# One piece of w_in, not four, multiplied in plain float32, and another table of moved works

## The chip, the cores and the metric

The kernel runs on one core of one Trainium2 chip. The metric is the device time of one execution in microseconds (us). A core has engines that work side by side and wait for each other by semaphores: TensorE (PE in the profile, with its weight loads as PEld), VectorE (DVE), ScalarE (ACT), GpSimd (POOL) and SyncE (SP), whose queue issues every load and store of this kernel.

## The reference

Attention over 4 batches and 12 heads of 448 positions and width 64, causal, and then two dense layers on its output, with an ELU between them:

```python
scores = scale * np.matmul(q, k.transpose(0, 1, 3, 2))
scores = np.where(mask, -1000000000.0, scores)
attn = softmax(scores)                      # rows, with 1e-9 in the sum
attn_out = np.matmul(attn, v)
x = attn_out.transpose(0, 2, 1, 3).reshape(B * S, H * D)   # 1792 x 768
h = x @ w_in                                # 768 x 2048
g = np.where(h > 0.0, h, np.exp(np.minimum(h, 0.0)) - 1.0)
out = g @ w_out                             # 2048 x 768
```

The weights come as float64 and are turned into float32 on the core.

## The kernel before

**Tiling.** The 448 positions of a batch are cut into four chunks of 112. A token tile is one chunk index of all four batches, 448 columns; the first tile (g = 0) needs only the first chunk of queries and keys, the second one two chunks, the last two tiles ("joint") three or four. Heads are taken in six pairs p, since two heads fill 128 partitions. w_in is cut into 16 pieces f of 128 output columns, each with six blocks k of 128 rows, and block k of the first layer meets the output of head pair k.

**Stages.** `first_pair` does the attention of the first tile for one pair: loads (q0, k0, and v0 in two halves), scores `sc` (L515), softmax on VectorE (L419) and ScalarE (L423), transposes `tr` (L440), products with v `av` (L453), the spread of the reciprocal sums `rb` (L535), and `xf`, the normalised float32 result (L539). `attention(0)` and `attention(1)` do the same for the second tile and for the last two (L614, L679, L647). `layers(g)` is the first dense layer of tile g, `mixed_h` that of the last two tiles and `mixed_o` the second layer of two tiles each.

**A piece of w_in.** `load64` brings its float64 words (768 KB); `convert` makes float32 of them in five steps on VectorE and ScalarE (L736, L740, L741, L744, L747) and stores them to `kin` (L758). `in_two` then splits the piece into a high and a low part `whl`: a copy in the rounded type (L775 on ScalarE, or L776 on VectorE) and a subtraction (L778, VectorE). x is split likewise into `xh` and `xl`. A block product is then three matmuls of 448 columns in the rounded type (`three`, L817 to L819).

**PLAIN.** For tile 0 the first PLAIN pieces are not split: a block product is one float32 matmul of `xf` with the piece (L840; the trace shows two records for each). With PLAIN = 4 these are pieces 0 to 3, 24 matmuls. Pieces 0 to 2 run abreast (k outside, f inside), the others one after the other. `xf[k]` is given back after the last plain piece has met it.

**What sets the order.** Nothing is written out by hand. Every step is a "work" of a `Plan`, with an engine (or a choice of ScalarE and VectorE), an estimated cost, what it reads and writes, and a due time. `draft` places the works one after the other: of those that can start at about the same time on an engine the one wanted first is taken, and `want = due - SOONER[n]` for work number n. SOONER is the table of moved works. The order that results is fixed when the program is built; at run time each engine does its own list in that order and waits where an input is late. The same holds for the loads: SyncE issues them in the listed order, and each waits until the eighth before it has landed.

Of the kernel before, what the change touches and what calls it, by code (L numbers as in the profile page):

```python
# [108 lines left out]
class Plan:  # L109
# [21 lines left out]
    def add(self, ways, reads=(), writes=(), due=None, size=0.0, hold=(), after=None):  # L131
# [24 lines left out]
        return w  # L156

    SOONER = {
# [30 lines left out]
    }  # L189

    def rank(self):
# [124 lines left out]
def attention_moe_kernel(ctx, tc, qk, v, w_in, w_out, out):  # L316
# [42 lines left out]
    BANKS = ("hp", "p", "av", "bank")  # L359
    SHARED = {"row": sum(PLACES[x] for x in ROWS), "bank": sum(PLACES[x] for x in BANKS)}  # L360

    PLAIN = 4

    def ring(tag):
        if tag not in rings:
# [4 lines left out]
    def new(tag, shape, dtype=F32, name=None):  # L370
        pool = ps if tag in BANKS else sb
        slot = "row" if tag in ROWS else "bank" if tag in BANKS else tag
        bufs = SHARED.get(slot) or PLACES[slot]
        return ring(tag).new(lambda: pool.tile(shape, dtype, tag=slot, name=name or tag, bufs=bufs))

    def pe(cost, fn, reads, writes, due, hold=(), after=None):
        return plan.add(("PE", cost, fn, False), reads, writes, due, hold=hold, after=after)
# [29 lines left out]
    def done(*bufs):  # L407
        for b in bufs:
            b.ring.done(b)
# [356 lines left out]
    def in_two(w, n):  # L766
        t = new("w6", [P, 2, KT, P], F32R, "whl")
        hi_lo(lambda: t()[:, 0, :n], lambda: t()[:, 1, :n], lambda: w()[:, :n], n * P, (t, 0), (t, 1), w)
        done(w)
        return t, (lambda k: t()[:, 0, k]), (lambda k: t()[:, 1, k])  # L770
# [55 lines left out]
    def emit_h(g, f, k, due):  # L826
        if k == 0:
            if g == 0:
                for n in range(0 if f == 0 else f + EARLY, min(f + EARLY + 1, FT)):
                    load64(("i", n))  # L830
                w = convert(("i", f))
            elif f < FT - BOTH:
                w = fetch(f)
            if g == 0 or f < FT - BOTH:
                st["w", f] = (w,) if g == 0 and f < PLAIN else in_two(w, KT)
            st["h", f] = new("hp", [P, S], name="hp")
        hp, w = st["h", f], st["w", f]
        if len(w) == 1:
            x = xf[k]
            pe(ONE, lambda: nc.tensor.matmul(hp(), w[0]()[:, k], x(), start=k == 0, stop=k == KT - 1), [*w, x], [hp], due)  # L840
            if f == PLAIN - 1:
                done(x)
        else:
            x = xt[g, k]
            pe(THREE, lambda: three(hp, w, k, x, k == 0, k == KT - 1), [w[0], *x], [hp], due)
            if f == (FT - 1 if g == 0 else FT - 1 - BOTH):
                done(*x)
        if k < KT - 1:
            return
        if g or f < FT - BOTH:  # L850
            done(w[0])
        o = G[0, f // HALF_F, g, f % HALF_F] = row("G")
        elu(o, hp)

    def layers(g):
# [4 lines left out]
        for f, k in order:  # L860
            yield ONE if g == 0 and f < PLAIN else THREE, lambda due, f=f, k=k: emit_h(g, f, k, due)

# [367 lines left out]
```

## Time and profile before

| what | us |
|---|---|
| median of three runs | 604.09 |
| lowest and highest run | 602.19, 604.17 |
| the profiled execution | 602.11 |
| its span, from the first instruction to the last | 600.3 |
| TensorE busy in it | 588.2 |
| VectorE busy | 517.3 |
| ScalarE busy | 440.6 |

The profile is of one execution. Its span leaves out some 1.8 us of the execution's own time. A view by stage shows where an engine idles; the chain of waits runs back from the last instruction to what released each step; the timeline lists instructions by start. TensorE's matmuls overlap their neighbours, so that the durations of single rows add up to more than the time; the chain and the distances between starts do not have that fault. The clock that TensorE was granted was 0.999 of full speed over the span.

### The profile page before, as it was taken

How to read it: one execution, taken by the hardware profiler on the slowest of the kernel's cores; microseconds unless marked ns; L12 is line 12 of the kernel's file. 1: busy time of each engine (PE TensorE's matmuls, PEld its weight loads, DVE VectorE, ACT ScalarE, POOL GpSimd, SP SyncE). 2: the span in 40 equal slices, each digit the busy share in tenths (PEclk: the TensorE clock that was granted, in tenths of full speed). 3: DMA queues.
4: the chain of work that ended last, by engine and by line, in shares of the span. 5: the costliest groups of instructions: out<-in, count | busy, mean ns of one | idle time of the engine just before them, and what ended most of it. 6: DMA issues, size and time to landing. Idle time of an engine off the chain costs nothing.

```text
span 600.3 us, 11631 instructions
## 1 busy us (share of the span) xinstructions
PE 588.2 (98%) x4086; PEld 518.2 (86%) x4086; DVE 517.3 (86%) x1212; ACT 440.6 (73%) x980; POOL 1.5 (0%) x12
## 2 busy tenths in 40 slices
PE   6999999999999999999999999999999999999997
PEld 5766888888788888888888889999999999999996
DVE  4889999999999999998999897699878999998511
ACT  6999989899899989887779766258747886574300
POOL 0000000000000000000000000000000000000000
PEclk9999999999999999999999999999999999999999
DMA  9999999988999999875456588996953334451111
GB/s 228 250 346 342 374 287 316 279 240 252 327 325 298 348 318 280 278 214 169 139 166 199 156 288 256 334 329 238 319 159 106 106 105 132 117 141 53 46 48 46
DMA packets 113610, 134.36 MB, mean 224 GB/s; under 512 B 42512, under 2 KB 86800, under 8 KB 113552
## 3 DMA queue, kind: packets, MB, share of 16 engines
q1 hardware_dynamic: 113552, 133.62, 72.2%
q8 instruction: 32, 0.52, 0.4%
q14 instruction: 26, 0.21, 0.1%
HBM read 101.45 MB, written 32.15 MB: 223 GB/s over the span
## 4 chain that ended last, share of the span: by engine, by line
PE 91%; DMA 2%; ACT 2%; SPq 2%; DVE 2%; issue 0%; ACTq 0%
PE op L817 12%; PE op L819 11%; PE op L818 11%; PE hp L817 11%; PE hp L819 10%; PE hp L818 10%; PE av L647 6%; PE tr L679 6%; PE sc L614 6%; PE hp L840 3%; DMA v<-in_v 1%; DMA w<-kin 1%; SPq L500 1%; PE av L453 1%; SPq L505 1%; ACT a L423 1%
## 5 line engine op out<-in xcount | busy, mean ns | idle before, releaser
L775 ACT ACTIVATE whl<-w 128x768 fp32r<-128x768 f32 x102 | 85.4, 842 | 75.5 <-PE op L819 41.2
L817 PE MATMUL op<-ph,whl 128*128 128x448 f32 (+1 forms) x338 | 126.4, 374 | 0.0
L819 PE MATMUL op<-ph,whl 128*128 128x448 f32 (+1 forms) x338 | 123.1, 364 | 0.0
L818 PE MATMUL op<-pl,whl 128*128 128x448 f32 (+1 forms) x338 | 123.1, 364 | 0.0
L778 DVE TENSOR_TENSOR whl<-w,whl 128x768 fp32r<-128x768 f32 x108 | 102.4, 953 | 14.4 <-ACT whl L775 14.0
L423 ACT ACTIVATE a<-a,nm 112x336 f32<-112x336 f32 (+3 forms) x192 | 98.0, 522 | 11.9 <-DVE nm L419 11.7
L419 DVE CUSTOM_DVE_ANT_0 a<-sc,mask 112x336 f32<-112x336 f32 (+3 forms) x192 | 74.7, 443 | 9.3 <-PE sc L515 7.4
L817 PEld LDWEIGHTS op<-ph,whl 128*128 128x128 f32 x338 | 63.5, 188 | 8.8 <-issue 3.8
L819 PEld LDWEIGHTS op<-ph,whl 128*128 128x128 f32 x338 | 63.5, 188 | 5.2
L818 PEld LDWEIGHTS op<-pl,whl 128*128 128x128 f32 x338 | 63.6, 188 | 4.5
L817 PE MATMUL hp<-xh,whl 128*128 128x448 f32 x168 | 65.6, 390 | 0.0
L819 PE MATMUL hp<-xh,whl 128*128 128x448 f32 x168 | 61.4, 366 | 0.0
L818 PE MATMUL hp<-xl,whl 128*128 128x448 f32 x168 | 61.4, 366 | 0.0
L818 PE MATMUL hp<-pl,whl 128*128 128x448 f32 x168 | 61.4, 365 | 0.0
L817 PE MATMUL hp<-ph,whl 128*128 128x448 f32 x168 | 61.4, 365 | 0.0
L819 PE MATMUL hp<-ph,whl 128*128 128x448 f32 x168 | 61.3, 365 | 0.0
L679 PE MATMUL tr<-ident,a 112*112 112x112 f32 x432 | 50.2, 259 | 0.5 <-DVE nm L419 0.4
L679 PEld LDWEIGHTS tr<-ident,a 112*112 112x112 f32 x432 | 45.1, 133 | 5.8 <-DVE nm L419 1.1
L683 ACT ACTIVATE at<-tr 112x448 f32<-112x448 f32 (+1 forms) x109 | 47.5, 497 | 1.5 <-PE tr L679 1.5
L647 PEld LDWEIGHTS av<-at,v 112*64 112x64 f32 x864 | 41.5, 137 | 5.5 <-issue 3.1
L647 PE MATMUL av<-at,v 112*64 112x112 f32 x864 | 45.4, 261 | 0.0
L913 ACT ACTIVATE m<-hp 128x448 f32<-128x448 f32 x56 | 30.2, 538 | 13.9 <-DVE hp L908 7.0
(96 smaller groups left out, 990.4 us busy)
## 6 DMA issues: line engine op xcount, KB each, us to landing
w<-kin SPq DMA_DIRECT2D x40, 384.0 KB, 5.4
w<-in_w_in SPq DMA_DIRECT2D x16, 768.0 KB, 9.1
w<-in_w_out SPq DMA_DIRECT2D x24, 512.0 KB, 6.3
w<-sout SPq DMA_DIRECT2D x32, 384.0 KB, 3.4
w<-kout SPq DMA_DIRECT2D x24, 384.0 KB, 3.2
qk<-in_qk SPq DMA_DIRECT2D x24, 336.0 KB, 5.3
kin<-w SPq DMA_DIRECT2D x16, 384.0 KB, 7.1
sout<-w SPq DMA_DIRECT2D x12, 512.0 KB, 5.6
```

The source lines that it names most:

```text
L419: plan.add(dve(n, lambda: nc.vector.tensor_tensor_reduce(out=a()[:, c], in0=sc()[:, c], in1=mask[:, S - n:], op0=ALU.add, op1=ALU.min, sca ...
L423: plan.add(act(n, lambda: nc.scalar.activation(a()[:, c], a()[:, c], AF.Exp, bias=nm()[:, x:x + 1], scale=-1.0, accum_out=su()[:, x:x + 1] ...
L614: nc.tensor.matmul(sc[half]()[:, lo:lo + n], s["q"](d, x), s["k"](d, y, n), start=i == 0, stop=i == len(s["split"]) - 1,)
L647: nc.tensor.matmul(av()[half_of(half), chunk(u % 4)], o["v"][1](half, i), at()[:, chunk(x)], start=i == 0, stop=i == chunks(u) - 1,)
L679: nc.tensor.transpose(tr()[:, chunk(x)], a[:, chunk(i)], ident)
L683: act(w, lambda: nc.scalar.activation(at()[:, :w], tr()[:, :w], AF.Copy)),
L775: act(n, lambda: nc.scalar.activation(h(), x(), AF.Copy), 0.09),
L778: sub = lambda eng: lambda: eng.tensor_tensor(out=l(), in0=x(), in1=f32(h()), op=ALU.subtract)
L817: nc.tensor.matmul(acc(), wh(k), xh(), start=first, stop=False, skip_group_check=more)
L818: nc.tensor.matmul(acc(), wh(k), xl(), start=False, stop=False, skip_group_check=more)
L819: nc.tensor.matmul(acc(), wl(k), xh(), start=False, stop=last, skip_group_check=more)
L913: plan.add(act(S, lambda: nc.scalar.activation(m(), h(), AF.Relu, scale=-1.0)), [h], [m])
```

## The change

PLAIN goes from 4 to 1, so that pieces 1, 2 and 3 are split for tile 0 like the others: 18 float32 matmuls go (24 to 6), 54 matmuls in the rounded type come, and three splits. `xf[k]` is given back after piece 0. Since the works are numbered in order of their making, and three splits are two works each, the numbers behind them shift; the table SOONER is another one, of 240 entries, and moves works all over the program.

```diff
     SOONER = {
-        0: 284.3, 1: 284.4, 7: -8.8, 12: 1.9, 14: -2.2, 15: -3.8, 17: 0.4, 21: -14.5, 23: -45.2, 31: 0.6,
...
+        0: 160.1, 1: 164.8, 2: 11.8, 3: 8.8, 5: -12, 6: 1.7, 10: 0.6, 15: -43, 16: -1.2, 21: -2.8, 29: 3.3, 32: 2,
...
     }
...
-    PLAIN = 4
+    PLAIN = 1
```

Lines behind the table stand four lines higher in the changed kernel (L840 is L836 there). Three places show what the table does.

**The loads at the start**, SyncE's queue. In the kernel before, from the sixth load on (q and k are the first tile's queries and keys of a pair, v a half of its values, w a piece of w_in):

```order
L500 DMA k_104<-in_qk 128x4x112
L505 DMA v_106<-in_v 112x4x64 x2
L500 DMA q_109<-in_qk 128x4x112
L500 DMA k_111<-in_qk 128x4x112
L505 DMA v_127<-in_v 112x4x64
L500 DMA q_129<-in_qk 128x4x112
L500 DMA k_131<-in_qk 128x4x112
L728 DMA w_133<-in_w_in 128x1536
L505 DMA v_151<-in_v 112x4x64 x2
L505 DMA v_127<-in_v 112x4x64
L500 DMA q_182<-in_qk 128x4x112
L500 DMA k_189<-in_qk 128x4x112
```

The same stretch of the changed kernel, down to the last of the first tile's queries:

```order
L724 DMA w_106<-in_w_in 128x1536
L496 DMA q_108<-in_qk 128x4x112
L496 DMA k_110<-in_qk 128x4x112
L501 DMA v_112<-in_v 112x4x64 x2
L496 DMA q_115<-in_qk 128x4x112
L501 DMA v_131<-in_v 112x4x64 x2
L724 DMA w_134<-in_w_in 128x1536
L496 DMA k_150<-in_qk 128x4x112
L724 DMA w_155<-in_w_in 128x1536
L501 DMA v_161<-in_v 112x4x64 x2
L496 DMA k_187<-in_qk 128x4x112
L496 DMA q_193<-in_qk 128x4x112
```

The first piece of w_in moved up from behind the fifth pair's q and k to the seventh place, and two more pieces now stand ahead of the last pair's q and k; before, one piece stood there.

**TensorE at the start**. In the kernel before, from the first product with v of a pair (`v_106`) to the first plain product `hp`:

```order
L453 MATMUL av<-at,v_106 64x112 x6
L535 MATMUL rb<-ident,rr_80 64x112 x8
L440 MATMUL tr<-ident,a 112x112 x8
L453 MATMUL av<-at,v_127 64x112 x8
L515 MATMUL sc<-k_131,q_129 112x112 x8
L440 MATMUL tr<-ident,a 112x112 x4
L535 MATMUL rb<-ident,rr_82 64x112 x8
L453 MATMUL av<-at,v_151 64x112 x8
L535 MATMUL rb<-ident,rr_83 64x112 x8
L440 MATMUL tr<-ident,a 112x112 x4
L515 MATMUL sc<-k_189,q_182 112x112 x8
L840 MATMUL hp<-xf,w 128x448 x2
```

In the changed kernel, from the fifth pair's scores on:

```order
L511 MATMUL sc<-k_150,q_115 112x112 x8
L436 MATMUL tr<-ident,a 112x112 x4
L531 MATMUL rb<-ident,rr_81 64x112 x8
L449 MATMUL av<-at,v_131 64x112 x8
L449 MATMUL av<-at,v_161 64x112 x4
L511 MATMUL sc<-k_187,q_193 112x112 x8
L531 MATMUL rb<-ident,rr_82 64x112 x8
L449 MATMUL av<-at,v_161 64x112 x2
L531 MATMUL rb<-ident,rr_83 64x112 x8
L449 MATMUL av<-at,v_161 64x112 x2
L531 MATMUL rb<-ident,rr_80 64x112 x8
L436 MATMUL tr<-ident,a 112x112 x16
```

The last pair's scores moved ahead of the products and spreads of the pairs before it, and no plain product stands near them any more: the first one comes two products with v and one group of second-tile scores after this stretch.

**TensorE around the plain products**, `hp` of the first pieces in the changed kernel:

```order
L449 MATMUL av<-at,v_229 64x112 x8
L836 MATMUL hp<-xf,w 128x448 x5
L813 MATMUL hp<-xh,whl 128x448
L814 MATMUL hp<-xl,whl 128x448
L815 MATMUL hp<-xh,whl 128x448
```

Where before the plain products of four pieces stood between the groups of the attention, five plain products of piece 0 now stand in a row, and split products of pieces 1 and 2 follow them at once.

## Rows read from the trace of the kernel before

**Rows 1.** The page: span; busy us, share of the span and instructions by engine.

```profile
span 600.3 us, 11631 instructions
PE 588.2 (98%) x4086; PEld 518.2 (86%) x4086; DVE 517.3 (86%) x1212; ACT 440.6 (73%) x980; POOL 1.5 (0%) x12
```

**Rows 2.** Busy by stage: window, length, each engine's busy us, clock, DMA share, GB/s.

```profile
20.00:40.00 20.00, 20.00 (x202) 13.80 (x198) 17.82 (x75) 19.36 (x54) 0.00 (x0) 1.00 1.04 323
40.00:60.00 20.00, 20.00 (x110) 12.63 (x105) 18.14 (x46) 18.73 (x46) 0.00 (x0) 1.00 1.05 335
...
80.00:100.00 20.00, 20.00 (x139) 17.98 (x137) 19.31 (x47) 18.38 (x42) 0.00 (x0) 1.00 0.99 258
100.00:120.00 20.00, 20.00 (x171) 17.51 (x170) 18.95 (x63) 16.37 (x45) 0.00 (x0) 1.00 0.96 301
...
140.00:160.00 20.00, 18.74 (x158) 15.90 (x156) 19.50 (x54) 17.44 (x41) 0.00 (x0) 1.00 0.89 278
```

**Rows 3.** The chain of waits, 11 to 57 us: start, length, what.

```profile
11.83 7.63 DMA v<-in_v
...
20.49 0.97 PE sc L515 x16
...
22.91 0.77 PE av L453 x16
...
25.94 1.70 PE hp L840 x4
...
29.62 0.95 PE hp L840 x2
...
35.05 3.96 PE hp L840 x10
...
43.31 8.46 PE hp L840 x22
...
56.42 0.21 PE hp L817
56.62 0.20 PE hp L818
56.83 0.20 PE hp L819
```

**Rows 4.** Timeline of SyncE's queue: start and length of an issue, in and out.

```profile
9.66 1.12 SPq L728 DMA_DIRECT2D w<-in_w_in  x1
...
23.93 1.78 SPq L728 DMA_DIRECT2D w<-in_w_in  x1
```

**Rows 5.** DMA issues of 23.9 to 24.0 us: count, KB each, us to landing.

```profile
w<-in_w_in SPq DMA_DIRECT2D x1, 768.0 KB, 8.1
```

**Rows 6.** DMA of the first 32 us: packets, volume, mean rate, packet sizes.

```profile
DMA packets 13370, 8.00 MB, mean 250 GB/s; under 512 B 12127, under 2 KB 12893, under 8 KB 13366
```

**Rows 7.** Timeline of TensorE, 157 to 161 us, with idle time and its releaser.

```profile
157.54 0.36 PE L819 MATMUL hp<-xh,whl 128*128 128x448 f32 x1
158.22 0.41 PE L614 MATMUL sc<-qkhl 64*112 64x336 f32 x2 [0.32 <-ACT qkhl L775]
159.44 1.18 PE L614 MATMUL sc<-qkhl 64*112 64x336 f32 x10 [0.82 <-DVE qkhl L778]
160.55 0.47 PE L817 MATMUL hp<-xh,whl 128*128 128x448 f32 x1
```

**Rows 8.** The same view, 173 to 176 us.

```profile
173.70 0.55 PE L679 MATMUL tr<-ident,a 112*112 112x112 f32 x4
174.65 0.59 PE L679 MATMUL tr<-ident,a 112*112 112x112 f32 x4 [0.41 <-DVE nm L419]
175.02 0.45 PE L817 MATMUL hp<-xh,whl 128*128 128x448 f32 x1
```

**Rows 9.** Groups by line: out<-in, count, busy us, mean ns, idle before.

```profile
L778 DVE TENSOR_TENSOR whl<-w,whl 128x768 fp32r<-128x768 f32 x108 | 102.4, 953 | 14.4 <-ACT whl L775 14.0
...
L776 DVE CAST whl<-w 128x768 fp32r<-128x768 f32 x6 | 3.3, 550 | 0.0
```

54 rows, old and new, of the table SOONER are left out of this document.

## The prediction

> **What bounds the kernel now.** I read the page first: TensorE is busy for 588.2 of 600.3 us, VectorE for 517.3, ScalarE for 440.6 [rows 1]. A matmul's row overlaps its neighbours, so this alone doesn't make TensorE the bound. The view by stage says more: from 20 to 140 us TensorE has no idle time, while ScalarE and VectorE have little (19.36 and 17.82 of 20 us in the second stage); the first gap of TensorE is 1.26 us at 140 to 160 [rows 2]. The chain of waits then gives what a matmul really takes, since its steps don't overlap. It runs through a load up to 19.46 us (11.83 + 7.63) and from there on TensorE alone to beyond 57 us, with no gap between its steps [rows 3]. So from 20 us on every us of TensorE's work counts in full, and so does every us by which it starts late. Two things hold it elsewhere: the loads of the first 20 us, and short waits for VectorE and ScalarE between 157 and 175 us.
>
> The loads are the second thing to read. The third piece of w_in is issued at 23.93 us and lands 8.1 us later, at 32.0 [rows 4, 5]: the queue is that far behind its issues, and the first 32 us bring 8.00 MB at 250 GB/s [rows 6]. What is put ahead in this queue delays what comes behind it.
>
> **The change, part by part.**
>
> *Matmuls.* In the chain the 24 plain products take 3 x 1.70 + 2 x 0.95 + 3.96 + 8.46 = 19.42 us (of the steps of two and four records one each stands in [rows 3]). Six stay: the changed order has five in a row and one alone, like the steps of 3.96 and 0.95, 4.91 us. So 14.51 us go. The 54 new matmuls are 18 groups of 0.21 + 0.20 + 0.20 = 0.61 us [rows 3], 10.98 us. A first matmul behind another kind of work takes some 0.1 us more (160.55 to 160.86 where 0.20 is usual, by the next start in that view), and the order has a few more such places. I take 3.4 us saved (3.2 to 3.5). It is all TensorE's own time, thus on the path.
>
> Beside it stands a rule that speaks against this. TensorE's weight loads are busy for 12.63 of 20 us at 40 to 60 us, where the plain products are, and 86% over the span [rows 1, 2]. The Trainium skill, "Perfetto Trace Analysis", section "Identifying the Most-Contended Engine", takes the busy share of weight loads and not that of matmuls as the measure of how full TensorE is. By it TensorE would have room in that stage, and the 3.4 us would be worth nothing. The chain, in which one matmul starts when the one before it is through, disagrees; I go by the chain.
>
> *Loads at the start.* Here the table costs something. The last pair's scores need q_193, and ahead of it the changed queue has, with itself, 12 q and k of 224 KB, 6 halves of v of 112 KB and 3 pieces of 768 KB: 5664 KB. Before, 3680 KB had landed by 19.46 us (10 q and k, 6 halves, 1 piece), and 7008 KB by 32.0 us (16, 10, 3) [rows 3, 4, 5]: 265 KB per us between them. The missing 1984 KB take 7.5 us, so q_193 lands at about 26.9 us. Bounds: at the mean of [rows 6], 244 KB per us, it is 27.6; if the small loads that are no longer ahead of it cost as much per KB as those of the first 19.46 us (189 KB per us, 7.1 us for 1344 KB off 32.0), it is 24.9. I keep 26.9, which rests on the same mixture.
>
> TensorE stands behind that load, because the scores are ahead of the spreads and products that could fill the time. By the two orders, before the last pair's scores it has done 5 groups of scores, 24 transposes, 20 products with v and 16 spreads. Before the change it had done 4, 24, 16 and 16 when it began the fifth pair's scores, at 20.49 us [rows 3]. The difference is one group of scores, 0.97, and four products, half of 0.77 [rows 3]: 1.36 us. So at the same point of its work TensorE is 26.9 - 20.49 - 1.36 = 5.1 us later (3.0 to 5.8), and since it has no gaps in the kernel before from there to 140 us, nothing gives this back in that stretch.
>
> *Splits and copies.* Three subtractions of 0.953 us and, as the counts by line have it, three rounded copies of 0.550 us more on VectorE [rows 9], 4.5 us; other copies change engine the other way, and by the counts of all forms VectorE gets 2.5 us more in all and ScalarE nearly nothing. It costs nothing where TensorE is held by loads; where VectorE holds TensorE it counts.
>
> *The waits at 157 to 175 us.* From the last matmul at 157.54 to the one at 160.55 lie 3.01 us; one matmul and a dozen scores are 0.20 + 1.27 of it (a dozen without a wait, by the starts of the same view), so 1.54 is lost. From 173.70 to 175.02 eight transposes take 1.32 where 0.70 is usual: 0.6 more [rows 7, 8]. With a like place of 0.3 at 153.6 us it makes 2.4 us. TensorE now comes there with 5.1 us more of idle time behind it, which the feeding engines have too. Against it stand VectorE's additions and the moved works: I added up, with mean durations by form, VectorE's work ahead of each of TensorE's waits and TensorE's own ahead of it. Between 150 and 180 us of TensorE's work the tightest place needs 2.8 us more of VectorE, relative to TensorE, than before. With VectorE's idle time unchanged 2.4 + 2.8 - 5.1 = 0.1 us of waiting is left. So 2.3 us of the waits go. The two ends: nothing goes (0), all goes (2.4).
>
> *The rest.* The order at the end (last products, stores) is the same in kind; I take nothing for it. Earlier return of `xf` frees places in the pool of rows; no wait of TensorE in the trace points there, so nothing.
>
> *Sum.* 600.3 - 3.4 + 5.1 - 2.3 = 599.7 us span; with the 1.8 us around it 601.5. The profiled execution, 602.11, is at the low end of the runs (602.19 to 604.17, median 604.09). Taken from the median the same -0.6 us gives 603.5. Neither level is better founded, so the number is the middle, 602.5.
>
> **The rivals.**
>
> *Faster: the late load is covered.* If q_193 lands at the early bound and the moved works also feed the middle, the head costs 3.0 and all 2.4 us of waits go: -2.8 us. With a little less of either, as when TensorE's other works at the start fill more of the time than I count, it is -3.4 us and more, the whole of the matmuls' saving: 598.7 from the profiled execution. For it: the table is a whole other arrangement, and 7.5 us of load time rest on a mean rate. Against: the scores block TensorE's list until the load is there, and head and middle trade against each other, since a TensorE that comes earlier to 157 us waits there for VectorE.
>
> *Slower: ScalarE holds TensorE from 35 to 120 us.* The splits of pieces 1 and 2 and of x stand some 20 us sooner than before. Adding up as above, ScalarE's work ahead of TensorE's waits exceeds TensorE's own by at most 0.9 us before, in the first 60 us of work, and by up to 2.6 after. With ScalarE's later start (its first softmax waits for a third load instead of a second) that is just covered by the 5.1 us: the margin is about half a us. It decides from the point where ScalarE idles longer than that; before, it idled 0.6 + 1.3 us at 20 to 60 and 1.6 + 3.6 at 80 to 120 us [rows 2]. If it idles as much, 7.1 us, what is left by 110 us is some 3.8 us of waiting: 601.5 + 3.8 = 605.3.
>
> *No gain from the matmuls*, by the rule on weight loads: 601.5 + 3.4 = 604.9, less than half a per cent above 602.11.
>
> That the change doesn't do what it says is excluded by the order: 6 plain products, 18 more groups of three.
>
> **How the numbers follow.** What a measurement of this kernel can tell from no change is about 0.5%, 3 us. The forecast (-0.6; with its bounds from -2.8 to +2.6) gets 0.57, the late load covered 0.17, ScalarE 0.16, no gain from the matmuls 0.05, and 0.05 is left for what I don't see, 0.02 of it faster and 0.03 slower. Faster by over 0.5%: 0.17 + 0.02 = 0.19. Slower: 0.16 + 0.03 = 0.19. Within: 0.62. The range goes from the forecast's low bound at the profiled execution, 602.1 - 2.8 = 599.3, to its high bound near the median's level, 606.0 (604.09 + 2.6 is 606.7, but that end needs all bounds at once); it takes in the ScalarE case at the profiled level and, of the faster one, the part down to -2.8.
>
> **What would show it.** Right: the chain of the changed kernel has 6 plain products at 4.9 us; its TensorE begins the last pair's scores at 26 to 28 us behind a wait for `q`, and the first plain product at 35 to 36 us instead of 25.9; idle time of TensorE in the first 30 us is 4 to 5 us more; at 150 to 180 us there is less than 1 us. Wrong in the head: those scores before 25.5 us. Wrong in the middle: TensorE idle for over 2 us anywhere between 35 and 200 us, with ScalarE or VectorE as releaser, which would make it slower. Wrong in the matmuls: groups of three at more than 0.65 us in the first 60 us.

## The result: slower by 0.8 to 1.0%

The changed kernel took 607.33 us (median of four runs, 607.22 to 609.25) against 604.13 us before; the ratio of the fast runs is 1.0082, 95% interval [1.0062, 1.0103] (the two medians alone give 1.0053). Measured once more, later, it was 608.48 against 602.3 us, 1.0105 [1.0081, 1.0128]. Predicted were 602.5 us, from 599.3 to 606.0: the time lies outside the range and on the slower side. The profiled execution took 607.24 us, 605.5 of it span, 5.2 more than before.

The page of the changed kernel, first its line of busy times (busy us, share of the span, instructions), which answers to [rows 1]:

```profile
span 605.5 us, 11711 instructions
PE 587.2 (97%) x4104; PEld 520.5 (86%) x4104; DVE 520.9 (86%) x1217; ACT 439.5 (73%) x981; POOL 1.5 (0%) x12
```

TensorE is busy for 1.0 us less, and the span is 5.2 us longer. VectorE got 3.6 us more work (2.5 were counted). The view by stage (window, length, busy us of PE, PEld, DVE, ACT, POOL, clock, DMA share, GB/s) says where TensorE idles; it answers to [rows 2]:

```profile
0.00:20.00 20.00, 11.77 (x134) 9.44 (x135) 10.29 (x76) 12.58 (x48) 1.47 (x12) 1.00 0.98 266
20.00:40.00 20.00, 17.77 (x198) 13.88 (x198) 17.59 (x65) 20.00 (x56) 0.00 (x0) 1.00 1.01 295
40.00:60.00 20.00, 20.00 (x170) 16.76 (x168) 18.71 (x57) 19.97 (x55) 0.00 (x0) 1.00 0.96 298
...
120.00:140.00 20.00, 20.00 (x146) 17.37 (x145) 16.03 (x42) 14.14 (x31) 0.00 (x0) 1.00 0.85 256
140.00:160.00 20.00, 20.00 (x171) 17.57 (x170) 19.52 (x52) 17.80 (x42) 0.00 (x0) 1.00 0.74 225
160.00:180.00 20.00, 19.10 (x150) 15.95 (x149) 18.20 (x42) 17.78 (x38) 0.00 (x0) 1.00 1.01 336
180.00:200.00 20.00, 17.87 (x148) 15.10 (x149) 19.41 (x52) 18.80 (x43) 0.00 (x0) 1.00 1.00 313
```

Four stages of before that were not shown ahead, in the same view:

```profile
0.00:20.00 20.00, 13.14 (x148) 11.40 (x150) 9.87 (x75) 14.34 (x56) 1.47 (x12) 1.00 0.98 216
...
120.00:140.00 20.00, 20.00 (x183) 17.29 (x183) 18.73 (x52) 18.53 (x49) 0.00 (x0) 1.00 0.88 248
...
160.00:180.00 20.00, 19.59 (x162) 17.04 (x159) 19.48 (x47) 17.57 (x38) 0.00 (x0) 1.00 1.01 331
180.00:200.00 20.00, 20.00 (x166) 17.54 (x165) 19.20 (x50) 18.93 (x44) 0.00 (x0) 1.00 0.97 310
```

In the first 40 us TensorE idles 8.23 + 2.23 us where it idled 6.86 + 0: 3.6 us more. The gap of 1.26 us at 140 to 160 us is gone, as forecast; in its place stand 0.90 and 2.13 us at 160 to 200. And at 120 to 140 us VectorE and ScalarE idle 3.97 and 5.86 us, before 1.27 and 1.47.

**The start.** TensorE's timeline of the changed kernel (start, length, instruction, and in brackets the idle time before it and its releaser), with the last pair's scores, the first plain products and the first groups of three:

```profile
23.12 1.07 PE L449 MATMUL av<-at,v 112*64 112x112 f32 x8 [1.01 <-DMA v<-in_v]
25.30 1.04 PE L511 MATMUL sc<-k,q 64*112 64x112 f32 x16 [1.10 <-DMA q<-in_qk]
...
34.59 4.03 PE L836 MATMUL hp<-xf,w 128*128 128x448 f32 x10
38.10 0.71 PE L813 MATMUL hp<-xh,whl 128*128 128x448 f32 x1
...
39.07 0.37 PE L813 MATMUL hp<-xh,whl 128*128 128x448 f32 x1
```

The load it waits for, in the chain of waits (start, length, what):

```profile
15.88 9.28 DMA q<-in_qk
```

It was issued at 15.88 and landed at 25.16 us; 26.9 was forecast. The five plain products and one group take 39.07 - 34.59 = 4.48 us; the forecast's prices give 3.96 + 0.61 = 4.57 [rows 3].

**The middle.** TensorE's waits from 60 to 260 us (engine, line, what ended the wait, sum in us, times, longest), first of the changed kernel, then of before:

```profile
PE tr L675 <- DVE nm L415: 1.8, 1, 1.8
PE hp L815 <- DVE whl L774: 0.9, 1, 0.9
PE op L813 <- DVE G L911: 0.2, 1, 0.2
```

```profile
PE sc L614 <- DVE qkhl L778: 0.8, 1, 0.8
PE tr L679 <- DVE nm L419: 0.4, 1, 0.4
PE sc L614 <- ACT qkhl L775: 0.3, 1, 0.3
```

The 1.8 us stand at 190.82 us: the transposes wait for a softmax step of VectorE that comes behind the conversions of w_out in VectorE's list, as its timeline shows:

```profile
187.48 0.42 DVE L732 TENSOR_SCALAR w<-w 128x512 f32<-128x512 f32 x1
...
189.64 0.69 DVE L743 CUSTOM_DVE_ANT_0 w<-w,w 128x1024 uint16<-128x1024 uint16 x1
190.25 0.50 DVE L415 CUSTOM_DVE_ANT_0 a<-sc,mask 112x336 f32<-112x336 f32 x1
```

This step reads scores, and TensorE had written them by 188.49 us: the last group of scores ahead of the wait starts at 186.96 and takes 1.53 us. In between VectorE works through conversions.

Some 55 us earlier both engines stood still for a load of w_out (timeline of SyncE's queue for its issue, then of VectorE and ScalarE):

```profile
127.70 0.58 SPq L724 DMA_DIRECT2D w<-in_w_out  x1
```

```profile
135.90 0.43 DVE L732 TENSOR_SCALAR w<-w 128x512 f32<-128x512 f32 x1 [2.69 <-DMA w<-in_w_out]
```

```profile
135.88 0.68 ACT L740 ACTIVATE w<-w 128x512 int32<-128x512 uint32 x1 [3.56 <-DMA w<-in_w_out]
```

This stall does not set the wait of 1.8 us. In five traces with this order (the result, its repetition, and the runs with the late load ahead, with shorter splits and with filled waits) VectorE stands for w_out between 1.02 and 2.69 us, and the wait at 190 us is 1.80 to 1.82 us in all of them. By these rows it comes from the order in VectorE's list; no run moved that softmax step.

**The sum.** The span grew by 5.2 us: some -3.3 from the matmuls, +3.6 of idle time in the first 40 us, +0.6 behind the last matmul (4.2 us, before 3.6), and the rest, some 4.3 us, between 40 us and the end. The -3.3 is an estimate: if each of TensorE's steps is given the usual distance between the starts of such steps, its work adds up to some 580.4 us, before 583.7; other ways to take the usual distance give 2.7 to 3.9. Of the rest the stages show 2.0 us as gaps: from 80 to 260 us they add up to 3.63, before 1.67. The others would be stalls that a row's overlap with its neighbour hides, as 1.14 of the 1.54 us were visible in [rows 7].

### The profile page after: what moved, and what is told of

Read it like the earlier page. It is cut to its first block, busy times and chain, and to the rows that moved or that the text cites. A ratio compares the mean times of both kernels' runs of the same rounds, so it can differ in the third digit from the quotient of the medians.

```text
span 605.5 us, 11711 instructions
## 1 busy us (share of the span) xinstructions
PE 587.2 (97%) x4104; PEld 520.5 (86%) x4104; DVE 520.9 (86%) x1217; ACT 439.5 (73%) x981; POOL 1.5 (0%) x12
## 4 chain that ended last, share of the span: by engine, by line
PE 74%; DMA 12%; DVE 6%; ACT 3%; SPq 3%; issue 1%; DVEq 0%; ACTq 0%
PE op L813 12%; PE op L815 11%; PE op L814 11%; PE hp L813 9%; PE hp L815 9%; PE hp L814 8%; PE av L643 6%; PE tr L675 5%; PE sc L610 4%; DMA k<-in_qk 3%; DMA R<-rdram 2%; DMA w<-in_w_out 2%; DVE a L415 2%; DMA q<-in_qk 2%; DMA kin<-w 1%; SPq L496 1%
## 5 line engine op out<-in xcount | busy, mean ns | idle before, releaser
L774 DVE TENSOR_TENSOR whl<-w,whl 128x768 fp32r<-128x768 f32 x111 | 105.3, 953 | 12.3 <-ACT whl L771 11.8
L813 PE MATMUL hp<-xh,whl 128*128 128x448 f32 x186 | 72.9, 392 | 0.1
L815 PE MATMUL hp<-xh,whl 128*128 128x448 f32 x186 | 68.4, 368 | 1.1 <-DVE whl L774 0.9
L814 PE MATMUL hp<-xl,whl 128*128 128x448 f32 x186 | 68.0, 366 | 0.0
L679 ACT ACTIVATE at<-tr 112x448 f32<-112x448 f32 (+1 forms) x113 | 49.5, 498 | 5.2 <-PE tr L675 5.1
L813 PEld LDWEIGHTS hp<-xh,whl 128*128 128x128 f32 x186 | 35.0, 188 | 7.4 <-issue 3.8
```

The source lines that it names most:

```text
L679: act(w, lambda: nc.scalar.activation(at()[:, :w], tr()[:, :w], AF.Copy)),
L774: sub = lambda eng: lambda: eng.tensor_tensor(out=l(), in0=x(), in1=f32(h()), op=ALU.subtract)
L813: nc.tensor.matmul(acc(), wh(k), xh(), start=first, stop=False, skip_group_check=more)
L814: nc.tensor.matmul(acc(), wh(k), xl(), start=False, stop=False, skip_group_check=more)
L815: nc.tensor.matmul(acc(), wl(k), xh(), start=False, stop=last, skip_group_check=more)
```

## The experiments

Two theories stood against each other at first. "Path": TensorE's work is the time, so that matmuls saved are time saved, and the late start and the waits in the middle took it back. "Feeders": TensorE is fed just in time by VectorE and ScalarE, so that a shorter TensorE gains nothing and more feeding work costs. Ratios are to the kernel before, run beside it.

**Shorter plain products, nothing else** (kernel before). Pieces 1 to 3 lose 104 of 448 columns in five of six products, some 2.7 us of TensorE.

```diff
-            pe(ONE, lambda: nc.tensor.matmul(hp(), w[0]()[:, k], x(), start=k == 0, stop=k == KT - 1), [*w, x], [hp], due)
+            n = 344 if f > 0 and k > 0 else S
+            pe(ONE, lambda: nc.tensor.matmul(
+                hp()[:, :n], w[0]()[:, k], x()[:, :n], start=k == 0, stop=k == KT - 1
+            ), [*w, x], [hp], due)
```

> The kernel before; the plain products of pieces 1 to 3 with k > 0 take 344 of 448 columns (the other columns lack these products), so that a piece costs TensorE what 18 split products cost: 18 x 0.15 = 2.7 us less in all, nothing else moved. Theory 'TensorE': its time counts in full from 20 us on, as the prediction has it: 2.5 to 2.7 us faster. Rival 'feeders': ScalarE and VectorE hand over pieces and scores no faster, TensorE waits instead, in the first 100 us or at 157 to 175 us: less than 1 us faster, and TensorE's idle time after 25 us is 2 us more.

602.01 against 602.02 us, 0.9997 [0.9987, 1.0008]: nothing of the 2.7 us arrives. The share of each engine in the chain of waits (DMA are transfers, loads and stores, and SPq their issues) shows why, first before, then with the shorter products:

```profile
PE 91%; DMA 2%; ACT 2%; SPq 2%; DVE 2%; issue 0%; ACTq 0%
```

```profile
PE 71%; ACT 11%; DMA 8%; DVE 5%; SPq 3%; issue 1%; DVEq 0%; ACTq 0%
```

From 18.66 us, where a load of a piece of w_in takes 8.27 us, to 154 us the chain now runs almost wholly along ScalarE, VectorE and transfers. So these were close behind TensorE and take over when it gets shorter. (In the run with less splitting, below, where TensorE's work ahead of 49 us is untouched, TensorE keeps 89% of the chain.) TensorE's waits from 20 to 260 us:

```profile
PE tr L679 <- DVE nm L419: 1.2, 2, 0.8
PE sc L614 <- DVE qkhl L778: 0.8, 1, 0.8
PE sc L614 <- ACT w L740: 0.6, 1, 0.6
PE rb L535 <- DVE rr L429: 0.6, 1, 0.6
PE sc L614 <- ACT qkhl L775: 0.3, 1, 0.3
PE hp L819 <- DVE whl L778: 0.3, 1, 0.3
```

Up to 61 us there are now waits for `rr`, `w` and `whl`, and the ones for `nm` grew from 0.4 to 1.2. The kernel before shows no wait at these places, but two rows each of its timeline show how near two of the inputs were (the input, then its use):

```profile
29.90 0.20 DVE L429 RECIPROCAL rr<-rr 112x8 f32<-112x8 f32 x1
...
30.50 0.32 PE L535 MATMUL rb<-ident,rr 112*64 112x112 f32 x2
```

```profile
59.78 0.96 DVE L778 TENSOR_TENSOR whl<-w,whl 128x768 fp32r<-128x768 f32 x1
...
60.87 0.40 PE L819 MATMUL hp<-xh,whl 128*128 128x448 f32 x1
```

`rr` was ready 0.4 us ahead of its use, `whl` 0.13 us. The wait for `rr`, at 31.34 us, is not the edit's work: it comes ahead of the first shortened product, which starts at 35.82 us or later. The run with less splitting, below, in which nothing is changed before 49 us, has it too:

```profile
PE rb L535 <- DVE rr L429: 0.8, 1, 0.8
```

So the margin of 0.4 us in one execution is a wait of 0.8 us in another. What can go with the shorter products is 1.7 us of waits: `w`, `whl` and the growth at `nm`. A gapless row of matmuls in the chain says that TensorE was not late; it does not say how late its inputs could have been.

**The splits' work, nothing else** (kernel before). Behind the conversions of pieces 1 to 3 VectorE makes the copy and the subtraction of a split into words that nobody reads, 4.5 us.

```diff
+            if key in MORE:
...
+                nc.vector.tensor_copy(h.bitcast(F32R), x)
+                nc.vector.tensor_tensor(out=l.bitcast(F32R), in0=x, in1=f32(h), op=ALU.subtract)
```

> The kernel before; behind the conversion of each of pieces 1 to 3 VectorE also makes the rounded copy and the difference that a split makes (0.55 + 0.95 us each, 4.5 us in all), into a scratch that nobody reads. Theory 'feeders': VectorE stands in TensorE's way here, 3 to 4.5 us slower. Rival 'covered', as the prediction has it: TensorE has no wait from 25 to 140 us, the additions are hidden there and show at 157 to 175 us at most: 0 to 2 us slower.

605.05 us, 1.0048 [1.0036, 1.0061]: +2.9 us of the 4.5 added. TensorE waits 1.2 us for `rr` (a wait of 0.8 there occurs without the added work too, as said), 0.8 for `w` at 40.71 us and 0.7 for `nm` at 42.83 us, where the trace of before has no wait.

**Both together** (kernel before): PLAIN = 1's load on the engines, in the old order and with the old loads.

> The kernel before with both halves of the change of PLAIN at once and no table: plain products of pieces 1 to 3 shortened to the time of split ones (2.7 us less TensorE), and the three splits' work added on VectorE (4.5 us more). Theory 'feeders': the shorter products are worth nothing here either, 2.5 to 3.5 us slower than the kernel before, as with the added work alone. Rival 'TensorE': the 2.7 us come off the 3 us of the added work, within 0.6 us of the kernel before.

606.83 against 602.3 us, 1.0075 [1.0058, 1.0092]: +4.5 us. So this stand-in for the change of PLAIN, without any moved work, already costs most of what the changed kernel loses (6.2 us beside it). It is harder on VectorE than the change itself: all 4.5 us stand on VectorE, which got 3.6 us more in the changed kernel, while ScalarE got 1.1 less. TensorE's waits from 20 to 260 us:

```profile
PE tr L679 <- DVE nm L419: 2.3, 2, 1.9
PE hp L850 <- DVE w L750: 1.4, 1, 1.4
PE rb L535 <- DVE rr L429: 1.1, 1, 1.1
```

**Less splitting at the old place** (kernel before). Pieces 4 to 6, split at 49 to 65 us, have one block of six split.

```diff
-                st["w", f] = (w,) if g == 0 and f < PLAIN else in_two(w, KT)
+                st["w", f] = (w,) if g == 0 and f < PLAIN else in_two(w, KT, 1 if g == 0 and f < 7 else None)
```

> The kernel before; the splits of pieces 4 to 6 for the first tile cover one block of six (the others' products are left out): VectorE and ScalarE do some 4 us less between 49 and 65 us, nothing is moved. Theory 'feeders' (their amount of work sets the pace from 25 us on): 1.5 to 3 us faster. Rival 'the first conversions': TensorE is held by ScalarE's and VectorE's work up to some 45 us only, and what they save later is covered by what they have done ahead: within 0.7 us.

601.84 us, 0.9992 [0.9977, 1.0006]. Feeding work taken away at 49 to 65 us gains nothing, while work added beside the first conversions, up to some 45 us, cost 2.9 us. Whether work added at 49 to 65 us would be free as well was not run.

**The changed kernel, with the plain products back.** Pieces 1 to 3 are split, but one plain product of the high parts takes the place of three: TensorE's time as with PLAIN = 4, all else as in the changed kernel.

```diff
+            if g == 0 and f < 4:
+                fn = lambda: nc.tensor.matmul(hp(), f32(w[1](k)), f32(x[0]()), start=k == 0, stop=k == KT - 1)
```

> The changed kernel, its order and its splits kept; the 18 split products of pieces 1 to 3 for the first tile are one plain product each, of the high parts (the low parts are left out). TensorE's work grows by 18 x 0.15 = 2.7 us. Theory 'TensorE': 2.5 to 2.7 us slower than the changed kernel. Rival 'feeders': the waits at 165 to 200 us shrink by as much: less than 1.5 us slower.

610.35 us, 1.0126 [1.0107, 1.0145]: 1.3 to 2.7 us above the two measurements of the changed kernel. The larger figure is clear of noise, the smaller is not. The result lies between the bounds set ahead and favours neither theory.

**The late load moved ahead** (changed kernel): piece 0 is issued behind the last pair's `q`.

```diff
+        n, to = [next(i for i, o in enumerate(order) if o[0].n == x) for x in (252, 185)]
+        order.insert(to, order.pop(n))
```

> The changed kernel; the load of piece 0 of w_in (768 KB) is issued behind the last pair's q, not ahead of it; nothing else is moved. q then lands some 3.7 us earlier (that piece took the queue from 18.71 to 22.43 us), the piece later. Theory 'load': TensorE's waits for v and q at 21.9 to 25.3 us go and nothing takes their place: 2.0 to 2.7 us faster. Rival 'ScalarE': ScalarE has no idle time from 13 us on, its work of piece 0 waits for the piece, and TensorE meets its first w_in product too early: not over 1 us faster, up to 1.5 us slower.

608.5 us, 1.0114 [1.0094, 1.0134]: no gain, also against executions of the changed kernel at a like granted clock (0.990 to 0.994 of full speed here; 607.22 to 610.0 us at 0.992 to 0.994 there). The wait for `q` is gone, and others stand in its place (TensorE's waits, in a trace whose clock is at 0.84 of full speed in the first 20 us):

```profile
PE rb L533 <- ACT w L738: 0.9, 1, 0.9
PE av L451 <- ACT at L441: 0.9, 1, 0.9
```

**The changed kernel again, and with shorter splits** of pieces 1 to 3 (one block of six):

> The changed kernel as it is, for comparison on the same chip as the runs beside it: 0.6 to 1.0% slower than the kernel before, as in its own runs.

> The changed kernel; the splits of pieces 1 to 3 for the first tile cover one block of six, and all six products take that block (the other blocks' products are left out). VectorE does some 2.2 us less for it (0.95 to some 0.2 us each), ScalarE or VectorE some 2 us less in copies; nothing is moved. Theory 'feeders' (their amount of work sets the pace): 1.5 to 3 us faster than the changed kernel. Rival 'order': what TensorE waits for in the changed kernel is the loads at the start and round trips at 165 to 205 us, which this work is not part of: within 0.7 us.

1.0105 [1.0081, 1.0128] and, with the shorter splits, 1.0119 [1.0100, 1.0139]. Taking the splits' time out again brings nothing here, though adding it cost 2.9 us in the old order. In this trace VectorE and ScalarE stand for w_out for 1.03 and 1.91 us, in that of the changed kernel run beside it for 1.39 and 2.27. The wait of 1.8 us ends at 189.83 us against 191.16, so the run is still 1.3 us ahead there; its span ends up at 607.1 against 606.6 us. What it saved is lost behind 190 us, and by what was not found.

**The waits filled with transposes** (changed kernel), since the clock granted to TensorE fell behind waits of some runs:

```diff
+            for _ in range(12 if p == NP - 1 else 0):
+                nc.tensor.transpose(sc[0]()[:, chunk(0)], ident, ident)
```

> The changed kernel; in three of TensorE's waits it does transposes of the constant into the tile that the waiting instruction then overwrites: 10 ahead of the third product tile (the wait for v at 21.9 us), 12 ahead of the last pair's scores (the wait for q), 18 between the transposes at 188.9 us. They take some 0.1 us each, less than the waits (1.0, 1.1 to 1.7, 1.8 us). Theory 'clock': in the changed kernel's second profile the granted clock fell to 0.67 of full speed at 28 to 32 us and to 0.69 at 192 to 196 us, right behind these waits; without idle time there it stays at 1.00, the mean clock is 0.998 or more and the kernel 1 to 2 us faster than the changed one (ratio to the kernel before 1.007 to 1.009). Rival 'waits': the clock is an accompaniment, 1.010 as in its last runs.

607.91 us, 1.0102 [1.0085, 1.0118]: the time is the same. The test is weak, though. Only the profiled execution kept the clock at 1.000, and it was the shortest, 606.44 us; the other three had 0.994 to 0.996 and took 607.6 to 608.31. And the third filling came behind its wait, which is still 1.81 us, and added 1.8 us of transposes. What says more is the profile of the result: the clock is at 1.00 in every stage shown, and the span is 5.2 us longer all the same. So the clock is not the main cause.

**Empty tables**, PLAIN = 4 and PLAIN = 1, and another table (506 entries) for PLAIN = 4:

> The kernel before with an empty table of moved works, for comparison with the next one. The table's worth is not known from any trace; 2 to 6 us slower than the kernel before.

> The changed kernel with an empty table of moved works, so that PLAIN 4 against 1 is compared with nothing moved by hand on either side. Theory 'feeders' (one plain piece costs VectorE and ScalarE three splits in the first 50 us and saves TensorE time that it can't use): 4 us or more slower than PLAIN 4 with an empty table. Rival 'table' (the new table alone makes the changed kernel slow): at most 1 us slower than PLAIN 4 with an empty table, or faster.

> The kernel before, PLAIN 4, with further entries in its table (506 for 278), by which the planner's own plan ends 0.6 us earlier. Theory 'feeders': only an order in which ScalarE and VectorE hand over earlier at 25 to 60 us and at 157 to 175 us is worth something; 0.3 to 1 us faster. Rival: the plan is not exact to half a us, within 0.3 us either way.

605.81 us (1.0076), 617.17 (1.0253 [1.0238, 1.0268]) and 607.3 (1.0084 [1.0063, 1.0105]). The last one was expected to gain and costs some 5 us, as much as the whole change, with PLAIN at 4 and nothing but the order redrawn. Taken alone the first two say that PLAIN = 1 costs 11.4 us, and the trace offers a reason. Raw words of a weight piece and its split parts share a pool of eight places, through which three pieces more now pass, and with PLAIN = 1 loads of weights wait for TensorE to be through with a split piece (waits of SyncE's queue, 60 to 170 us):

```profile
SPq L697 <- PE hp L788: 6.2, 3, 3.3
```

With PLAIN = 4 and an empty table this wait is not among its queue's. It does not go by PLAIN alone, however: the kernel before has 2.1 us of it, the changed kernel with its table none. ScalarE waits 6.2 us for w_out in the run of PLAIN = 1. That made the theory "places".

**Nine places against eight**, empty table, PLAIN = 1; v and w give up one place each in both, to make room.

```diff
-        q=2, k=3, v=5, a=8, at=8, m=2, ob=2, R=2, tt=2, row=44, w6=8, w=7, nm=4, su=4, rr=4, hp=3, p=4, av=1, bank=0,
+        q=2, k=3, v=4, a=8, at=8, m=2, ob=2, R=2, tt=2, row=44, w6=9, w=6, nm=4, su=4, rr=4, hp=3, p=4, av=1, bank=0,
```

> The changed kernel with an empty table, as in the run of PLAIN = 1 without a table (617.2 us; 1.0253), with nine places instead of eight in the pool that the raw float64 words of the weights and the split pieces share; one place fewer for v (4) and for w (6) makes the room. Theory 'places': three pieces more pass through this pool, so that the loads of w_out are issued late and ScalarE and VectorE wait for them at 120 to 180 us; with a ninth place they come earlier, and the time falls by more than 6 us against the run beside it with eight places, and ScalarE's wait for w_out (6.2 us) goes. Rival 'engines': the extra splits cost VectorE's and ScalarE's time wherever they stand; the ninth place gives less than 2 us, and the waits of ScalarE and VectorE on TensorE's path stay.

> The same kernel with eight places in that pool, and the same fewer places for v (4) and w (6). It tells what the fewer places cost by themselves. Both theories: within 3 us of the run of PLAIN = 1 without a table (617.2 us; 1.0253 of before).

610.51 against 625.78 us: 15 us for a place. But two points did not fit. ScalarE's wait for w_out stayed at 6.2 us, and the run with eight places was 8.6 us above its like with five and seven places for v and w.

**The same pair with PLAIN = 4**, where the ninth place should be worth little:

> PLAIN = 4 with an empty table, with the same nine places in the shared pool and four for v and six for w as in the run of PLAIN = 1 with nine places. Theory 'places': with PLAIN = 4 three pieces fewer pass through the pool, no load of weights waits there for a product, and the ninth place is worth less than 3 us against the run beside it with eight places. Rival 'any order': a change of places draws a new order, and orders without a table differ by up to 15 us whatever the places are; then the pair differs by more than 3 us, in either direction.

> The same with eight places in the shared pool. Theory 'places': within 3 us of the run with nine places and near the 605.8 us of PLAIN = 4 without a table. Rival 'any order': further than 3 us from either.

619.03 us with nine places (1.0293 [1.0262, 1.0325]) and 608.81 with eight (1.0120): the ninth place costs 10 us here. The rival is right: a change of one size draws a whole new order, and orders without a table differ by 10 to 15 us in either direction. With that neither the 15 us nor the 11.4 us between the empty tables shows anything about places or about PLAIN.

**Nine places with a table made for them**, PLAIN = 1:

> PLAIN = 1 with nine places in the shared pool (four for v, six for w) and a table made for that. If the places are what the changed kernel lacks, it comes below the changed kernel (1.0082 to 1.0105 of before) by 2 us or more, and loads of weights no longer wait for PE's products; a gain against before would need the late start (3.3 us) and the splits beside the first conversions (3 us) to go too, so 602 to 606 us is expected. Rival 'engines': not below the changed kernel.

608.86 us, 1.0111 [1.0088, 1.0133], not below the changed kernel, though its stages show fewer gaps:

```profile
0.00:20.00 20.00, 13.47 (x148) 11.48 (x150) 10.68 (x77) 14.10 (x54) 1.47 (x12) 1.00 0.98 245
20.00:40.00 20.00, 16.86 (x173) 12.50 (x168) 18.43 (x74) 18.75 (x50) 0.00 (x0) 1.00 1.01 296
...
160.00:180.00 20.00, 19.22 (x157) 16.51 (x155) 18.19 (x45) 16.39 (x38) 0.00 (x0) 1.00 0.99 317
180.00:200.00 20.00, 19.95 (x162) 17.02 (x163) 18.14 (x46) 18.82 (x44) 0.00 (x0) 1.00 1.00 306
```

TensorE idles 0.83 us at 160 to 200 us, where the changed kernel idles 3.03, and 9.67 us in the first 40 us instead of 10.46. Yet the span of the profiled execution is 604.8 against 605.5 us: up to 580 us there are 2.3 us of gaps less (11.8 against 14.1), and they are worth 0.7. It is another order, so that this supports no theory of the places, and it warns against taking the sum of the gaps for the loss. No kernel of this study beat the one before.

## Why the prediction was wrong, step by step

**"It is all TensorE's own time, thus on the path"** is the step that failed. The size was about right (3.4 forecast, some 3.3 by the trace), its worth was not: 2.7 us off the same products give 0.9997. The chain of [rows 3] follows one engine while nothing else is later; inputs that were ready 0.1 to 0.4 us ahead of their use don't show in it. With the shorter products the chain leaves TensorE (71% of the span for 91%). The prediction read "no gap" as room for VectorE and ScalarE, though they were at 17.82 and 19.36 of 20 us [rows 2].

The rival "no gain from the matmuls" had the right number for this term at a chance of 0.05. The Trainium skill, "Perfetto Trace Analysis", section "Identifying the Most-Contended Engine", by which the weight loads' busy share (beside the share of the peak arithmetic rate) says how full TensorE is, gives that result as the prediction read it, and the run agrees with it (weight loads at 13.49 of 20 us at 40 to 60 us in that run). But matmul time added to the changed kernel came out 1.3 to 2.7 us slower, with weight loads at 12.03 of 20 us there. If that holds (the smaller figure is within the noise), the share of weight loads alone does not decide.

**The splits.** Counted at nothing "where TensorE is held by loads; where VectorE holds TensorE it counts". The second half held: the work of three splits beside the first conversions cost 2.9 us, and with the shorter products 4.5 (the first experiments). The prediction never priced this at the start, because it saw no wait of TensorE for VectorE between 20 and 153 us.

**The head.** The mechanism was right: the scores wait for `q`, the first plain product starts at 34.59 us. The size was not: 25.30 instead of 26 to 28 us. By the prediction's own sign (before 25.5 us) that is wrong in the head. The small loads that are no longer ahead cost 1344 KB / (32.0 - 25.16) = 196 KB per us, the early bound's price (189), not the mean's (265). Idle time grew by 3.6 us, inside the bounds of 3.0 to 5.8, below the 5.1. What was not seen is that the late start is no term of its own. With the load moved ahead TensorE waits for ScalarE instead, and the time stays.

**The middle.** "So 2.3 us of the waits go" failed. The waits of 140 to 160 us went, and larger ones came at 165 to 200: 2.13 us of idle time at 180 to 200, over the 2 us that the prediction named as its sign of being wrong there. The step rested on sums of VectorE's work ahead of each wait and on "VectorE's idle time unchanged". That idle time rose from 1.27 to 3.97 us at 120 to 140 us, 2.69 of it for one load of w_out, but the wait of 1.8 us is as long where the stall is 1.0 us. By the timeline it is made by conversions ahead of a softmax step in VectorE's list, and a sum over everything ahead of a wait cannot see whether such a step could have come sooner.

**The rival "ScalarE holds TensorE"** came nearest in time, 605.3 against 607.24 us, but not in place: ScalarE has not a gap at 20 to 40 us (20.00 busy), yet TensorE's gaps from 40 to 120 us are 0.17 us. The chain of the changed kernel says a little more for it and then something else: it leaves TensorE at 28.43 us, runs along ScalarE to 37.7, then along VectorE, from 43.28 to 92 us mostly along transfers (loads of `k`, the reciprocal sums' way through DRAM, a store of converted w_in), and is back on TensorE at 94.87. Its shares:

```profile
PE 74%; DMA 12%; DVE 6%; ACT 3%; SPq 3%; issue 1%; DVEq 0%; ACTq 0%
```

What the changed kernel lacks is not one engine's time.

**What is shown and what stays open.** Shown in a fixed order: 2.7 us less matmul time is worth nothing, the splits' work beside the first conversions costs 2.9 us, and the stand-in for PLAIN = 1 with both costs 4.5 us [3.5, 5.5]. The changed kernel loses 5 to 6 us. How much of that is PLAIN and how much the table stays open, since another table with PLAIN = 4 lost some 5 us as well. Taking away the splits' time or the wait for `q` leaves the changed kernel's time where it was, and the runs with other places changed too much at once to decide anything. That transfers hold the changed kernel from 43 to 92 us is read from its chain and was not tested.

## What to carry to other kernels

Before you book a saving on the busiest engine in full, subtract, place by place, the time at which each of its inputs was ready from the time at which it was used: where that is some tenths of a us, the saving ends there. A cheap test is to shorten the work itself and nothing else, and to see whether the chain of waits still runs along that engine. And where a program's order is drawn by a planner, two of its orders differ by up to 15 us for no reason in the change, so that a cause is tested in a fixed order or not at all.

## What was not expected of the hardware

Behind waits of 1.6 to 1.9 us the clock granted to TensorE fell in some executions of the same kernel and not in others. Stages of the changed kernel run again, then of the profiled execution of the result:

```profile
28.00:32.00 4.00, 4.00 (x48) 3.85 (x45) 2.36 (x11) 2.66 (x9) 0.00 (x0) 0.67 1.10 352
188.00:196.00 8.00, 6.18 (x34) 5.37 (x33) 7.86 (x20) 7.97 (x18) 0.00 (x0) 0.79 0.99 319
```

```profile
28.00:32.00 4.00, 4.00 (x60) 3.47 (x54) 3.11 (x13) 4.00 (x14) 0.00 (x0) 1.00 1.08 375
188.00:196.00 8.00, 5.87 (x35) 4.32 (x32) 7.86 (x20) 8.00 (x18) 0.00 (x0) 1.00 1.00 308
```

At 28 to 32 us 0.67 is a mean of stretches at 2.4 and 1.2 GHz. The same steps, from the spreads behind the last pair's scores to the products behind the next transposes, take 4.51 us in the result's profile (26.27 to 30.78) and 6.17 us with the slow stretch in them (26.54 to 32.71). Some of that 1.7 us may arrive at the end: the four executions of the changed kernel with a mean clock of 0.996 to 0.998 took 606.58 to 607.41 us, the six with 0.992 to 0.994 took 607.22 to 610.0. No run sets the clock by itself, so this is an association. It may be part of why the second measurement of the loss (6.2 us) is larger than the 5.2 us between the profiles; it is not why there is a loss.
